# A fused attention and mixture kernel: copies and casts of the first heads on other engines, a new plan, pools in another order

## The chip, the cores and the metric

The kernel runs on one core of one Trainium2 chip. Times are device microseconds of one execution. The kernel before took 740.96 us (median of 3 runs, 740.37 to 741.18). A profile was taken of one more execution; all rows below are from it.

## The reference

Three stages follow each other. The input has 4 batches of 8 heads, 576 tokens, head size 64.

```python
scores = scale * np.matmul(q, k.transpose(0, 1, 3, 2))
bias = -(cum[:, :, :, None] - cum[:, :, None, :])      # cum: running sum of max(s, 0)
scores = np.where(causal, -1e9, scores + np.minimum(bias, 0.0))
attn = np.exp(scores - scores.max(-1)); attn /= attn.sum(-1) + 1e-9
x = (attn @ v), heads side by side                     # 2304 tokens x 512
h = np.maximum(np.maximum(x @ w1, x @ w2), x @ w3)     # 768 columns
x = h @ w_out                                          # 512 columns
e_idx = argmax(x @ w_gate + modality_bias[modality_id])
out[mask] = gate_w[mask] * (np.maximum(x[mask] @ w1[e], 0) @ w2[e])   # 8 experts, 1024 columns
```

All matmuls work with split numbers: a value is a rounded high part (fp32r) and the rest as a low part, and three matmuls (high by high, low by high, high by low) make one product.

## The kernel before, in words

**Attention.** The 32 heads go one after the other, two of them (a pair) sharing one product with v. For each head: k and q come by DMA (L357, L358); their high parts are cast on ScalarE (`k_high` L386, `q_high` L389), k is copied to a second tile on GpSimd (`k_again` L392), the low parts are subtracted (`k_low` L396 on VectorE for head 0 and else on GpSimd, `q_low` L399 on GpSimd, tile q_b). TensorE makes the scores in six blocks (L406, L407), VectorE adds the mask and finds the least (L415), ScalarE takes exp (L422). TensorE then turns the probabilities in four banks of PSUM (L427), and each bank is copied to a tile pt in SBUF (`turned` L432), on VectorE for the (bank, head of the pair) pairs in `PT_V`, on ScalarE for the others: four and four of a pair's eight. The pair's product with v (L462, called pv here) goes to PSUM and is scaled into x (L468, L472).

**Fills.** Between these, TensorE gets pieces of the next stage: for later batches a part of the product of x with w1, w2, w3 is made during attention. A piece is three matmuls (L248, L249, L250; 288 columns); four pieces make one block of PSUM (two banks are there for them), which ScalarE copies (L501) or VectorE takes the maximum of (L503); a transfer h_d<-h (L506) writes the result to DRAM. What isn't made between the heads is made behind the last head.

**The order of the attention stage** is written by a planner, `planned()`: every step is a job with an engine, a guess of its time in ns (`SC_NS`, `PT_NS` and the like), what it waits for and which buffers it takes; among the jobs that could start soon on an engine the one with the lowest key goes first. A key is head x `KEY["T"]` plus a number for the kind of step. The jobs are issued in that order, engine by engine, and each engine works in order.

**Conversion of weights.** The 24 blocks of w1, w2, w3 and w_out come as 64-bit numbers (L212, 512 KB) and are converted: a shift of exponents on ScalarE (L224), three steps on VectorE (L226, L228, L230), a cast to the high part w_h (L235 on ScalarE), the low part w_l by subtraction (L237). Nine are jobs of the planner. The other 15 (`convert_rest`) are written behind the attention; their tiles are in the pools w2p and w1p, their raw data in rawp and raw2. These, and all that follows, are put in order by the framework's own scheduler.

**Behind attention** the first product goes on in six windows of 384 tokens (`stage_a`: L248 to L250 with 384 columns, copies L708, L709, L710, split L714, L715 into tiles fh, fl of the pool hp; x is split at L686, L687 into the pool xsp), then w_out (L724 to L726), routing, and the experts. Their pools are opened after those of attention are closed, on the same memory, one behind the other in the order in which they are written; a tile that lies over a tile of attention waits until that one was last used. The pools of attention lie in the order fxp (12 tiles xh, xl of the fills), fhp (2 tiles h of the fills), qkp (k and q), at1 (mask, q_b, e), vp, ss, tp (pt). The pools behind it are x2p, hmp, jkp, rp, mtp, unp, w2p, xsp, w1p, raw2, hp.

Of the kernel before, what the change touches and what calls it, by code (L numbers as in the profile page):

```python
# [16 lines left out]
T = B * S  # L17
# [64 lines left out]
MIN_NS = {(0, 0): 145, (1, 0): 278, (2, 0): 410, (3, 0): 545, (4, 0): 375, (4, 1): 400}  # L82
SC_NS = {(0, 0): 224, (1, 0): 224, (2, 0): 298, (3, 0): 408, (4, 0): 266, (4, 1): 266}
PT_NS = {"ACT": [420, 420, 275, 485], "DVE": [540, 540, 340, 605]}
CK_POOL = ()
KL_DVE = (0,)
C_ORDER = [(4, 0), (3, 0), (4, 1), (2, 0), (1, 0), (0, 0)]
T_ORDER = [1, 0, 3, 2]
PT_V = [(1, 0), (3, 0), (0, 1), (2, 1)]
CONV = [(0, 3), (1, 3), (2, 5), (3, 7), (4, 7), (5, 9), (6, 13), (7, 15), (8, 17)]  # L90
W_READY, SET_H = 15000, 24
WIRE_FROM, WIRE_TO, WIRE_SLOW = 1300, 900, 1.0
KEY = {"s3": 42741, "T": 27649, "wl": -69055, "wz": -30147, "w1": 173831, "wd": 76793, "ws": 297833, "lx": 64832, "lv": 72681, "ck": -58191, "kb": -116628, "kl": 170828, "ql": -15070, "s": 62000, "mn": 34943, "ex": 51, "ds": 799, "t": 1582, "dt": 3342, "cp": -245871, "r1": -66726, "r2": -76846, "rt": -27814, "rc": -105783, "rw": -81963, "pv": -100422, "x": 41915, "xc": 72719, "xs": 121384, "fe": 59240}
R_MOE1 = (2, 4, 7)
R_MOE2 = (1, 3, 5)

# [84 lines left out]
def fused_kernel(tc, qk, vd, sd, w64, mod, wg, wgt, mb, we, cst, csi, out):  # L181
# [3 lines left out]
    with top:  # L185
# [73 lines left out]
        with ExitStack() as es:  # L259
# [85 lines left out]
            def job(name, run, eng, ns, key, **k):  # L345
                j = Job(run, eng, ns, key, **k)
                jobs.append(j)
                st[name] = j
                return j

            def at(h, what, n=0):
                return h * KEY["T"] + KEY[what] + n

# [47 lines left out]
            def scores(h, c, k):  # L401
                hl, k_b, q_b = tl["hl", h], tl["k_b", h], qbs[h % QB_N]
                q0, w = QC[c][0], QC[c][2]
                k0, n = (k * 288, 288) if c == 4 else (0, w)
                s_ps = tl["s_ps", h, c, k] = ps_s.tile([128, 512], F32, name="s_ps")[:, 0:n]
                P.matmul(s_ps, hl[:, 1, q0:q0 + 128], hl[:, 0, k0:k0 + n], start=True, stop=False)  # L406
                P.matmul(s_ps, q_b[:, q0:q0 + 128], k_b[:, k0:k0 + n], start=False, stop=True)  # L407
# [21 lines left out]
            def turned(h, i):  # L429
                pt = tl["pt", h, i] = tp.tile([128, 512], F32, tag="pt", name="pt", bufs=PT_BUFS)  # L430
                a, z = BANKS[i][1:]
                (V.tensor_copy if (i, h % 2) in PT_V else A.copy)(out=pt[:, a:z], in_=tl["t_ps", h, i][:, a:z])  # L432

            def sums(p):
                r = tl["r", p] = ss.tile([128, 10], F32, name="r")
# [84 lines left out]
            for h in range(2 * NP):  # L520
# [15 lines left out]
                ex = {}  # L536
                for n, (c, k) in enumerate(C_ORDER):
                    bank = Slot("s")
                    a = job(("s", h, c, k), lambda h=h, c=c, k=k: scores(h, c, k), "PE", SC_NS[c, k] + 40, at(h, "s", n * KEY["ds"]), after=[kl, cq, kb, ql, lk], takes=[bank], uses=[s_h, s_q, s_k], tail=210)
                    a = job(("mn", h, c, k), lambda h=h, c=c, k=k: least(h, c, k), "DVE", MIN_NS[c, k], at(h, "mn", n * KEY["ds"]), after=[a] + ([st["mn", h, *C_ORDER[0]]] if n else []), takes=[s_e] if n == 0 else [], uses=[bank, s_e], lag=145 * k)  # L540
                    if k or c < 4:
                        ex[c] = job(("ex", h, c), lambda h=h, c=c: expo(h, c), "ACT", EXP_NS[c], at(h, "ex", n * KEY["ds"]), after=[a], uses=[s_e], tail=0)
                done += ex.values()
                for n, i in enumerate(T_ORDER):
                    bank, s_t = Slot("t"), Slot("pt")
                    turns = job(("t", h, i), lambda h=h, i=i: turn(h, i), "PE", 109 * len(BANKS[i][0]) - 82, at(h, "t", n * KEY["dt"]), after=[ex[c] for c in sorted({c for c, _ in BANKS[i][0]})] + [turns] * (turns is not None), takes=[bank], uses=[s_e], tail=247)
                    eng = "DVE" if (i, j) in PT_V else "ACT"
                    s_p.append((s_t, job(("cp", h, i), lambda h=h, i=i: turned(h, i), eng, PT_NS[eng][i], at(h, "cp", n * KEY["dt"]), after=[turns], takes=[s_t], uses=[bank])))
                if j:
                    bank, s_r, s_0, s_o = Slot("t"), Slot("rb"), Slot("t"), Slot("o")  # L550
# [38 lines left out]
        rp = top.enter_context(tc.tile_pool(name="rp", bufs=2, reuse_waits="tile"))  # L589
        mtp = top.enter_context(tc.tile_pool(name="mtp", bufs=N_EARLY + 2, reuse_waits="tile"))  # L590
        unp = top.enter_context(tc.tile_pool(name="unp", bufs=1, reuse_waits="tile"))
        w2p = top.enter_context(tc.tile_pool(name="w2p", bufs=12, reuse_waits="tile"))
        xsp = top.enter_context(tc.tile_pool(name="xsp", bufs=2, reuse_waits="tile"))
        w1p = top.enter_context(tc.tile_pool(name="w1p", bufs=W1_BUFS, reuse_waits="tile"))
        raw2 = top.enter_context(tc.tile_pool(name="raw2", bufs=R2_BUFS, reuse_waits="tile"))
        hp_ = top.enter_context(tc.tile_pool(name="hp", bufs=1, reuse_waits="tile"))
        ps_a = top.enter_context(tc.tile_pool(name="ps_a", bufs=5, space=PSUM, reuse_waits="tile"))
        ps_b = top.enter_context(tc.tile_pool(name="ps_b", bufs=2, space=PSUM, reuse_waits="tile"))
        ps_r = top.enter_context(tc.tile_pool(name="ps_r", bufs=1, space=PSUM, reuse_waits="tile"))
# [465 lines left out]
```

## Time and profile before

| what | value |
|---|---|
| median of 3 runs | 740.96 us |
| profiled execution, its own time | 743.25 us |
| span in its profile, first to last instruction | 741.5 us |
| mean granted clock of TensorE | 0.990 |
| TensorE matmul rows, share of the span | 97% |
| VectorE, ScalarE, GpSimd, shares of the span | 67%, 55%, 30% |
| attention with its fills ends | some 267 us after the start |

PE is TensorE's matmul row, PEld its weight loads, DVE VectorE, ACT ScalarE, POOL GpSimd, SP the engine that issues most transfers. A q behind a name is the engine's queue of instructions.

### The profile page before, as it was taken

What the parts mean: (1) busy time and instruction counts of PE and PEld (TensorE: products, weight loads), DVE (VectorE), ACT (ScalarE), POOL (GpSimd) and SP (SyncE); (2) the same over time, 40 slices, a digit from 0 to 9 for tenths busy, and PEclk for the clock granted to TensorE, in tenths of its full rate; (3) what the DMA queues carried; (4) which work ended last, traced back from release to release, by engine and by line L of the source; (5) the groups of instructions that cost most, each with busy time, mean ns of one, the idle gap of its engine ahead of it and who ended that gap; (6) DMA issues with size and microseconds to landing.
All of it is one profiled execution on the core that took longest, in us unless ns stands there. A gap on an engine that the chain in (4) does not pass through costs nothing. (4 is left out here: it accounts for less than half of the span.)

```text
span 741.5 us, 13641 instructions
## 1 busy us (share of the span) xinstructions
PE 715.7 (97%) x4602; PEld 639.0 (86%) x4602; DVE 495.2 (67%) x1536; ACT 404.7 (55%) x992; POOL 224.4 (30%) x233
## 2 busy tenths in 40 slices
PE   4999999999999998999999999999999999999996
PEld 4787888778899997999999998999899988999885
DVE  5878988786641158969687796765776566575540
ACT  6999999898721134522222222546555665565531
POOL 7688879766201200000010111032221212222101
PEclk9999999999999999999999999999999999999999
DMA  7576666763131004411101011668478565666610
GB/s 213 152 204 194 205 189 193 198 178 113 64 122 43 31 23 151 146 67 13 53 12 64 23 49 51 202 164 274 123 233 276 203 233 194 233 215 213 226 44 19
DMA packets 43535, 103.83 MB, mean 140 GB/s; under 512 B 9472, under 2 KB 13472, under 8 KB 43456
## 3 DMA queue, kind: packets, MB, share of 16 engines
q1 hardware_dynamic: 35808, 86.04, 37.3%
q0 software_dynamic: 4912, 11.82, 5.0%
q10 hardware_dynamic: 2736, 5.01, 1.8%
q8 instruction: 38, 0.62, 0.4%
q14 instruction: 41, 0.34, 0.2%
HBM read 88.83 MB, written 12.18 MB: 136 GB/s over the span
## 5 line engine op out<-in xcount | busy, mean ns | idle before, releaser
L248 PE MATMUL a_ps<-xh,w_h 128*128 128x384 f32 (+2 forms) x492 | 159.7, 327 | 2.1 <-ACT w_h L235 1.5
L250 PE MATMUL a_ps<-xh,w_l 128*128 128x384 f32 (+2 forms) x492 | 156.9, 320 | 1.6 <-DVE w_l L237 1.4
L249 PE MATMUL a_ps<-xl,w_h 128*128 128x384 f32 (+2 forms) x492 | 156.5, 319 | 0.0
L767 DVE TENSOR_TENSOR e_l<-e_raw,e_h 128x512 fp32r<-128x512 f32 x160 | 104.0, 689 | 11.4 <-ACT e_h L766 10.1
L766 ACT CAST e_h<-e_raw 128x512 fp32r<-128x512 f32 x160 | 93.0, 622 | 14.0 <-DMA e_raw<-in_we 6.0
L248 PEld LDWEIGHTS a_ps<-xh,w_h 128*128 128x128 f32 x492 | 92.8, 189 | 4.4 <-ACT w_h L235 1.9
L250 PEld LDWEIGHTS a_ps<-xh,w_l 128*128 128x128 f32 x492 | 93.0, 189 | 3.3 <-DVE w_l L237 2.8
L249 PEld LDWEIGHTS a_ps<-xl,w_h 128*128 128x128 f32 x492 | 93.2, 189 | 1.0 <-POOL xl L490 0.2
L675 POOL DMA_INDIRECT table<-meta,si x18 | 19.4, 1080 | 244.7 <-DVE nm L663 149.6
L422 ACT ACTIVATE e<-e,mn 128x448 f32<-128x448 f32 (+4 forms) x160 | 88.4, 555 | 4.2 <-DVE mn L415 4.2
L797 PE MATMUL h_ps<-x2t,e_h 128*128 128x256 f32 x288 | 81.1, 282 | 0.0
L798 PE MATMUL h_ps<-x2t,e_l 128*128 128x256 f32 x288 | 81.0, 282 | 0.0
L796 PE MATMUL h_ps<-x2t,e_h 128*128 128x256 f32 x288 | 80.6, 283 | 0.0
L427 PE MATMUL t_ps<-ident,e 128*128 128x128 f32 x480 | 73.5, 288 | 2.8 <-DVE pt L432 2.0
L406 PE MATMUL s_ps<-hl 128*128 128x288 f32 (+1 forms) x192 | 66.7, 357 | 7.8 <-DVE hl L396 7.1
L650 DVE CUSTOM_DVE_ANT_0 junk<-x,wg 128x512 bf16<-128x512 f32 x96 | 66.0, 687 | 11.8 <-ACT x L728 11.0
L415 DVE CUSTOM_DVE_ANT_0 e<-s_ps,mask 128x288 f32<-128x288 f32 (+4 forms) x160 | 63.2, 423 | 14.2 <-PE s_ps L407 13.1
L427 PEld LDWEIGHTS t_ps<-ident,e 128*128 128x128 f32 x480 | 58.8, 148 | 7.7 <-DVE pt L432 2.7
L407 PE MATMUL s_ps<-k_b,q_b 66*128 66x288 f32 (+1 forms) x192 | 59.6, 323 | 4.6 <-DMA k_b<-augk 3.3
L826 PE MATMUL y_ps<-e_h,gh 128*128 128x512 f32 x152 | 61.5, 405 | 0.4 <-ACT gh L818 0.4
L828 PE MATMUL y_ps<-e_h,gl 128*128 128x512 f32 x152 | 60.8, 400 | 0.0
L827 PE MATMUL y_ps<-e_l,gh 128*128 128x512 f32 x152 | 60.1, 395 | 0.0
(178 smaller groups left out, 1488.8 us busy)
## 6 DMA issues: line engine op xcount, KB each, us to landing
e_raw<-in_we SPq DMA_DIRECT2D x80, 512.0 KB
w_raw<-in_w SPq DMA_DIRECT2D x24, 512.0 KB
qk_r<-in_qk SPq DMA_DIRECT2D x31, 288.0 KB
v_r<-in_vd SPq DMA_DIRECT2D x16, 320.0 KB
rb<-r_d SPq DMA_DIRECT2D x32, 160.0 KB
qk_r<-in_qk SPq DMA_DIRECT2D x32, 144.0 KB
x2d<-x ACTq DMA_DIRECT2D x18, 256.0 KB
w_h<-w_z POOLq DMA_DIRECT2D x9, 256.0 KB, 3.8
```

The costliest lines, as they stand in the source:

```text
L248: P.matmul(a_ps, wh[:, c], xh, start=c == 0, stop=False)
L249: P.matmul(a_ps, wh[:, c], xl, start=False, stop=False)
L250: P.matmul(a_ps, wl[:, c], xh, start=False, stop=c == 3)
L406: P.matmul(s_ps, hl[:, 1, q0:q0 + 128], hl[:, 0, k0:k0 + n], start=True, stop=False)
L422: A.activation(out=ec, in_=ec, func=ACTF.Exp, bias=tl["mn", h][:, c:c + 1], scale=-1.0, accum_out=tl["l", p][:, j, c:c + 1])
L427: P.transpose(out=t_ps[:, n * 128:(n + 1) * 128], in_=e_bufs[h % E_N][:, EOFF[c] + kb * 128:EOFF[c] + (kb + 1) * 128], identity=ident)
L650: V.tensor_tensor_reduce(out=junk, in0=x2, in1=wg_sb[ei // 2][:, ei % 2, :], scale=1.0, scalar=0.0, op0=ALU.mult, op1=ALU.add, accum_out=l ...
L766: A.copy(out=h, in_=raw[:, a])
L767: V.tensor_tensor(out=lo, in0=raw[:, a], in1=h.bitcast(F32), op=ALU.subtract)
L796: P.matmul(h_ps, w(hs, f, c), xt[:, 0, c], start=c == 0, stop=False)
L797: P.matmul(h_ps, w(hs, f, c), xt[:, 1, c], start=False, stop=False)
L798: P.matmul(h_ps, w(ls, f, c), xt[:, 0, c], start=False, stop=c == 3)
```

## The change

Three things change. For the first six heads two more banks of each pair, (0, 0) and (1, 1), are copied by VectorE, so six of eight. The cast of k for heads 3 and 5 goes from ScalarE to GpSimd. The planner's table of keys is another one, and its guess for the scores is 30 ns longer; so all steps of attention are ordered anew. The pools behind attention lie in another order: hp and xsp come before w2p, and hp no longer last.

```diff
-CK_POOL = ()
+CK_POOL = (3, 5)
...
+PT_EARLY, PT_W = 6, [(0, 0), (1, 1)]
...
-KEY = {"s3": 42741, "T": 27649, "wl": -69055, "wz": -30147, "w1": 173831, "wd": 76793, "ws": 297833, "lx": 64832, "lv": 72681, "ck": -58191, "kb": -116628, "kl": 170828, "ql": -15070, "s": 62000, "mn": 34943, "ex": 51, "ds": 799, "t": 1582, "dt": 3342, "cp": -245871, "r1": -66726, "r2": -76846, "rt": -27814, "rc": -105783, "rw": -81963, "pv": -100422, "x": 41915, "xc": 72719, "xs": 121384, "fe": 59240}
+KEY = {"s3": 262888, "T": 15750, "wl": 29386, "wz": 48740, "w1": 225687, "wd": 68498, "ws": 411529, "lx": 95995, "lv": 209700, "ck": 138477, "kb": -116340, "kl": -53033, "ql": -58361, "s": 115494, "mn": -5610, "ex": 153024, "ds": 361, "t": 18694, "dt": 19213, "cp": -53151, "r1": -208485, "r2": -212716, "rt": 15596, "rc": -242689, "rw": 44183, "pv": -165391, "x": -56845, "xc": 100720, "xs": -74110, "fe": -88191}
...
-                (V.tensor_copy if (i, h % 2) in PT_V else A.copy)(out=pt[:, a:z], in_=tl["t_ps", h, i][:, a:z])
+                (V.tensor_copy if (i, h % 2) in PT_V or h < PT_EARLY and (i, h % 2) in PT_W else A.copy)(out=pt[:, a:z], in_=tl["t_ps", h, i][:, a:z])
...
-                    a = job(("s", h, c, k), lambda h=h, c=c, k=k: scores(h, c, k), "PE", SC_NS[c, k] + 40, at(h, "s", n * KEY["ds"]), after=[kl, cq, kb, ql, lk], takes=[bank], uses=[s_h, s_q, s_k], tail=210)
+                    a = job(("s", h, c, k), lambda h=h, c=c, k=k: scores(h, c, k), "PE", SC_NS[c, k] + 70, at(h, "s", n * KEY["ds"]), after=[kl, cq, kb, ql, lk], takes=[bank], uses=[s_h, s_q, s_k], tail=210)
...
-                    eng = "DVE" if (i, j) in PT_V else "ACT"
+                    eng = "DVE" if (i, j) in PT_V or h < PT_EARLY and (i, j) in PT_W else "ACT"
...
         unp = top.enter_context(tc.tile_pool(name="unp", bufs=1, reuse_waits="tile"))
+        hp_ = top.enter_context(tc.tile_pool(name="hp", bufs=1, reuse_waits="tile"))
+        xsp = top.enter_context(tc.tile_pool(name="xsp", bufs=2, reuse_waits="tile"))
         w2p = top.enter_context(tc.tile_pool(name="w2p", bufs=12, reuse_waits="tile"))
-        xsp = top.enter_context(tc.tile_pool(name="xsp", bufs=2, reuse_waits="tile"))
         w1p = top.enter_context(tc.tile_pool(name="w1p", bufs=W1_BUFS, reuse_waits="tile"))
         raw2 = top.enter_context(tc.tile_pool(name="raw2", bufs=R2_BUFS, reuse_waits="tile"))
-        hp_ = top.enter_context(tc.tile_pool(name="hp", bufs=1, reuse_waits="tile"))
```

One line comes in near the top, so a step at line n of before is at n + 1 in the changed kernel.

On ScalarE, behind the last copy of probabilities (pt): before, the copies of the fills (L501) and of the first projected block (L708) come first, and then the first cast of the 15 conversions (w_h).

```order
L432 COPY pt<-t_ps 128x512
L686 CAST xh<-x_2825 128x384 x4
L501 COPY h<-a_ps 128x288
L486 CAST xh<-x_1270 128x288 x2
L486 CAST xh<-x_2066 128x288 x2
L501 COPY h<-a_ps 128x288 x3
L486 CAST xh<-x_2066 128x288 x4
L501 COPY h<-a_ps 128x288 x2
L486 CAST xh<-x_2066 128x288 x2
L501 COPY h<-a_ps 128x288 x2
L708 COPY h<-a_ps 128x384 x2
L235 CAST w_h<-w_z 128x512
```

The same place in the changed kernel:

```order
L433 COPY pt<-t_ps 128x512
L236 CAST w_h<-w_z 128x512 x2
L225 ACTIVATE w_z<-w_raw 128x512 x2
L236 CAST w_h<-w_z 128x512
L502 COPY h<-a_ps 128x288
L687 CAST xh<-x_2875 128x384
L236 CAST w_h<-w_z 128x512
L487 CAST xh<-x_1269 128x288 x2
L225 ACTIVATE w_z<-w_raw 128x512
L487 CAST xh<-x_2055 128x288 x2
L236 CAST w_h<-w_z 128x512
```

The conversions moved in among the fills' copies; all 15 casts w_h stand ahead of the copy of the first projected block.

On VectorE, from the last pair's x to the first maximum of a projected block (L709), before:

```order
L468 TENSOR_TENSOR x_2825<-o_ps,rb 128x512
L503 TENSOR_TENSOR h<-a_ps,h 128x288
L472 TENSOR_TENSOR x_2825<-t_ps,rb 128x64
L687 TENSOR_TENSOR xl<-x_2825,xh 128x384
L503 TENSOR_TENSOR h<-a_ps,h 128x288 x17
L709 TENSOR_TENSOR h<-a_ps,h 128x384 x2
```

The end of the same stretch in the changed kernel:

```order
L231 SCALAR_TENSOR_TENSOR w_z<-w_raw,w_z 128x512
L504 TENSOR_TENSOR h<-a_ps,h 128x288
L227 TENSOR_SCALAR w_z<-w_z 128x512
L238 TENSOR_TENSOR w_l<-w_z,w_h 128x512
L229 SCALAR_TENSOR_TENSOR w_z<-w_raw,w_z 128x512
L231 SCALAR_TENSOR_TENSOR w_z<-w_raw,w_z 128x512
L504 TENSOR_TENSOR h<-a_ps,h 128x288 x2
L238 TENSOR_TENSOR w_l<-w_z,w_h 128x512
L504 TENSOR_TENSOR h<-a_ps,h 128x288 x4
L710 TENSOR_TENSOR h<-a_ps,h 128x384 x2
```

Seventeen evictions of fills stood by themselves; now the steps of the conversions stand between them, and four evictions follow the last w_l.

On GpSimd, at the start of attention, with buffer numbers (q_b0 to q_b2 are of heads 0 to 2, hl_194 is head 1's, hl_204 head 2's), before:

```order
L399 TENSOR_TENSOR q_b0_124<-qk_r_169,hl_182 64x576
L399 TENSOR_TENSOR q_b1_125<-qk_r_174,hl_194 64x576
L399 TENSOR_TENSOR q_b2_126<-qk_r_177,hl_204 64x576
L396 TENSOR_TENSOR hl_194<-qk_r_174,hl_194 64x576
L396 TENSOR_TENSOR hl_204<-qk_r_177,hl_204 64x576
L392 CAST k_b_228<-qk_r_177 64x576
L396 TENSOR_TENSOR hl_276<-qk_r_213,hl_276 64x576
```

and now (hl_274 is head 3's):

```order
L400 TENSOR_TENSOR q_b0_124<-qk_r_169,hl_182 64x576
L400 TENSOR_TENSOR q_b1_125<-qk_r_174,hl_194 64x576
L397 TENSOR_TENSOR hl_194<-qk_r_174,hl_194 64x576
L400 TENSOR_TENSOR q_b2_126<-qk_r_177,hl_204 64x576
L397 TENSOR_TENSOR hl_204<-qk_r_177,hl_204 64x576
L387 CAST hl_274<-qk_r_213 64x576
L393 CAST k_b_228<-qk_r_177 64x576
L397 TENSOR_TENSOR hl_274<-qk_r_213,hl_274 64x576
```

Head 1's low half of k moved ahead of head 2's q_b, and the cast of k for head 3 has come in. On TensorE, counted in the order: ahead of the sixteenth pv stand 67 pieces of fills before and 71 now.

## Rows read from the trace of the kernel before

**Rows 1.** The page, part 1: busy us, share of span, instructions of each engine.
```profile
PE 715.7 (97%) x4602; PEld 639.0 (86%) x4602; DVE 495.2 (67%) x1536; ACT 404.7 (55%) x992; POOL 224.4 (30%) x233
```

**Rows 2.** Windows: length, busy us (instructions) of PE, PEld, DVE, ACT, POOL; clock, DMA.
```profile
20.00:60.00 40.00, 38.43 (x256) 30.16 (x254) 33.40 (x115) 37.32 (x107) 30.50 (x29) 0.91 0.62 170
60.00:213.00 153.00, 149.17 (x1150) 124.72 (x1149) 120.71 (x405) 132.04 (x386) 102.71 (x91) 0.99 0.55 161
213.00:268.00 55.00, 54.41 (x389) 52.31 (x388) 11.12 (x25) 8.84 (x24) 7.78 (x10) 1.00 0.18 61
```

**Rows 3.** Windows of 10 us behind the fills, the same columns.
```profile
280.00:290.00 10.00, 7.98 (x43) 7.02 (x41) 8.09 (x15) 4.70 (x9) 0.00 (x0) 0.98 0.48 158
290.00:300.00 10.00, 8.92 (x40) 8.13 (x41) 9.00 (x18) 5.44 (x9) 0.00 (x0) 0.84 0.51 156
```

**Rows 4.** Groups by line of PE, 268 to 301: busy, mean ns, idle before.
```profile
L248 PE MATMUL a_ps<-xh,w_h 128*128 128x384 f32 x52 | 18.4, 353 | 2.0 <-ACT w_h L235 1.5 <-ACT h L708 0.5
L250 PE MATMUL a_ps<-xh,w_l 128*128 128x384 f32 x51 | 18.2, 357 | 1.6 <-DVE w_l L237 1.4
L249 PE MATMUL a_ps<-xl,w_h 128*128 128x384 f32 x52 | 18.0, 346 | 0.0
```

**Rows 5.** Timeline of PE: start us, length, instruction; two of 45 close starts.
```profile
268.19 0.34 PE L249 MATMUL a_ps<-xl,w_h 128*128 128x384 f32 x1
...
275.96 0.34 PE L248 MATMUL a_ps<-xh,w_h 128*128 128x384 f32 x1
```

**Rows 6.** Timeline of ACT: first copy of a projected block, first cast w_h, fh0.
```profile
267.37 0.86 ACT L708 COPY h<-a_ps 128x384 f32<-128x384 f32 x2 [2.71 <-PE a_ps L249]
271.60 0.62 ACT L235 CAST w_h<-w_z 128x512 fp32r<-128x512 f32 x1 [3.36 <-DMA h_d<-h]
272.12 0.51 ACT L714 CAST fh<-h 128x384 fp32r<-128x384 f32 x1
```

**Rows 7.** Groups of DVE by shape, 280 to 300: the conversion's steps.
```profile
L228 DVE SCALAR_TENSOR_TENSOR w_z<-w_raw,w_z 128x512 int32<-128x512 int32 x6 | 4.1, 689 | 0.1
L237 DVE TENSOR_TENSOR w_l<-w_z,w_h 128x512 fp32r<-128x512 f32 x6 | 4.1, 688 | 0.3 <-ACT w_h L235 0.2
...
L226 DVE TENSOR_SCALAR w_z<-w_z 128x512 int32<-128x512 int32 x6 | 2.6, 425 | 1.9 <-ACT w_z L224 1.8
```

**Rows 8.** Groups by shape, 213 to 268: VectorE's evictions of fills.
```profile
L503 DVE TENSOR_TENSOR h<-a_ps,h 128x288 f32<-128x288 f32 x18 | 8.2, 458 | 41.9 <-PE a_ps L250 33.7 <-issue 5.2 <-ACT h L501 3.0
```

**Rows 9.** Timeline of DVE: the last pair's x, and the xl behind it.
```profile
216.99 0.21 DVE L472 TENSOR_TENSOR x<-t_ps,rb 128x64 f32<-128x64 f32 x1
217.78 0.56 DVE L687 TENSOR_TENSOR xl<-x,xh 128x384 fp32r<-128x384 f32 x1 [0.58 <-ACT xh L686]
```

**Rows 10.** Groups of ACT, 264 to 302: the conversion's steps.
```profile
L235 ACT CAST w_h<-w_z 128x512 fp32r<-128x512 f32 x10 | 6.2, 618 | 7.2 <-DVE w_z L230 3.7 <-DMA h_d<-h 3.4
L224 ACT ACTIVATE w_z<-w_raw 128x512 f32<-128x512 f32 x9 | 6.1, 677 | 6.6 <-DVE w_l L237 3.6 <-DMA w_raw<-in_w 3.0
```

**Rows 11.** Groups of DVE by shape, 20 to 200: a conversion step during attention.
```profile
L228 DVE SCALAR_TENSOR_TENSOR w_z<-w_raw,w_z 128x512 int32<-128x512 int32 x11 | 14.7, 1344 | 0.1
```

**Rows 12.** Groups by shape, 20 to 60: the copies and casts that change engine.
```profile
L392 POOL CAST k_b<-qk_r 64x576 fp32r<-64x576 f32 x8 | 6.3, 797 | 0.2
L386 ACT CAST hl<-qk_r 64x576 fp32r<-64x576 f32 x7 | 4.7, 669 | 0.2
...
L432 DVE COPY pt<-t_ps 128x448 f32<-128x448 f32 x6 | 3.7, 623 | 1.7 <-PE t_ps L427 1.2 <-ACT e L422 0.5
L432 ACT COPY pt<-t_ps 128x448 f32<-128x448 f32 x5 | 2.6, 523 | 0.8 <-PE t_ps L427 0.8
```

**Rows 13.** Waits, 20 to 60: who, for whom, us in total, times, longest.
```profile
POOL hl L396 <- ACT hl L386: 6.9, 3, 4.7
```

**Rows 14.** Timeline of POOL: low halves of k, heads 1 and 2.
```profile
12.20 2.79 POOL L396 TENSOR_TENSOR hl<-qk_r,hl 64x576 fp32r<-64x576 f32 x2
```

**Rows 15.** Timeline of PE: head 1's first block of scores.
```profile
14.00 0.58 PE L406 MATMUL s_ps<-hl 128*128 128x288 f32 x1
```

## The prediction

> **What bounds the kernel now.** I read the page first, then the stretches in windows, then who waited for whom in the two places where the windows show a loss. By the page TensorE's matmul row is busy 97% of the span [rows 1], so a first guess is that nothing on the other engines matters. The windows correct that. From 213 to 268 us the matmuls stand close while VectorE works 11.1 us of 55 and ScalarE 8.8 [rows 2]; this is the stretch in which the fills that are left run by themselves. Straight behind it, in 280 to 300, the number of matmuls falls to 43 and 40 in 10 us while VectorE works 8.1 and 9.0 us [rows 3]. So the kernel has 55 us with two nearly empty engines, and then a place where TensorE waits for just these two.
>
> How much is lost there? Between 268 and 301 us the three lines of the projection ran 52 + 51 + 52 = 155 matmuls of 384 columns [rows 4]. Close together they start 0.177 us apart: two starts 44 matmuls apart are 275.96 - 268.19 = 7.77 us [rows 5]. 155 x 0.177 = 27.4 us of 33, so 5.6 us are lost. The releasers named are the weights' conversion, w_h on ScalarE and w_l on VectorE [rows 4]; at the same place the granted clock is 0.84 in one window [rows 3], a part of it at the lower level, 1.2 GHz in place of 2.4.
>
> Here the measure decides the size. The busy shares of the matmul row in 280 to 300 leave 20 - 7.98 - 8.92 = 3.1 us [rows 3]; counted, it is 5.6. The Trainium skill (Perfetto Trace Analysis, "Identifying the Most-Contended Engine") says that matmul busy time is no good measure and points to the LDWEIGHTS busy share instead. By that share (7.02 + 8.13 in the two windows [rows 3], against 52.3 of 55 in the fills [rows 2], 9.5 in each) the loss would be 3.9 us, and my sum would end 1.7 us higher. The trace agrees on the first half of the rule; on the second the count of matmuls says more, because a load at the lower clock is itself longer.
>
> Why were the conversions late? ScalarE's first w_h stands at 271.60 and had waited 3.36 us for the landing of a fill's transfer h_d<-h [rows 6], issued at the end of the last fill. The first tile of the pool w2p lies over memory of the fills' last tiles. Since ScalarE works in order, all 15 conversions that the planner doesn't hold stand behind it.
>
> **The change part by part.** *Pools in another order.* hp and xsp now lie where w2p began, and w2p over tiles that the last heads free. The order shows what this lets loose: in ScalarE's row all 15 casts w_h now stand ahead of the copy of the first projected block, where before all stood behind it. The 5.6 us go; ends 3.1 (busy shares) and 5.6. What is late next is the fills' own end: fh0 now lies where that last fill tile was, and needs the landing that released the cast at 271.60; its cast stood at 272.12 anyway, behind that one [rows 6], so this costs nothing.
>
> The conversions now share VectorE's row with the evictions of the fills. From the last pair's x to the last w_l the new row has 13 w_l, 12 + 11 of the two three-operand steps, 11 shifts and 12 fill evictions: 13 x 0.688 + 23 x 0.688 + 11 x 0.425 [rows 7] + 12 x 0.458 [rows 8] + one xl 0.56 [rows 9] = 35.5 us. Behind it stand four evictions of VectorE, so six of fills, each 12 matmuls, 1.7 us at the 389 in 55 us of [rows 2]: 10.2 us. Together 45.7 us, against the 50 us that TensorE's own work took there before, from x at 217.2 [rows 9] to the first projected copy at 267.4 [rows 6]. ScalarE adds 15 x 0.618 + 13 x 0.677 = 18.1 us [rows 10] to 8.8 of 55 and isn't near. If VectorE runs without a gap, TensorE waits for nothing; if it is kept at 85%, as in 280 to 300 (17.1 of 20 [rows 3]), 35.5 / 0.855 + 10.2 = 51.7, 1.7 us too many. Ends 0 and 10 (the step that takes 689 ns there took 1344 on average in the attention stage [rows 11]; 11 x 0.655 = 7.2 more, also at 85%). I take +1.0: GpSimd's work beside it is 7.8 us of 55 [rows 2].
>
> That 1344 has a rule beside it that speaks against the change. The Trainium skill (SBUF — State Buffer, "Who interferes with whom") says that a VectorE instruction with two inputs in SBUF contends with GpSimd instructions that read SBUF. By it each of the fills' ten xl on GpSimd would meet a conversion; the doubled step in attention agrees. If all ten cost the 0.65 us, the 45.7 us would be 52.2, and the sum would end 2.2 us higher than at no gap.
>
> *Copies and casts of the first six heads.* Six copies of 448 columns leave ScalarE, 6 x 0.523 = 3.1 us, and cost VectorE 6 x 0.623 = 3.7; two casts of k leave ScalarE, 2 x 0.669 = 1.3, and cost GpSimd 2 x 0.797 = 1.6 [rows 12]. In 20 to 60 us ScalarE was the fullest, 37.3 of 40, VectorE 33.4, GpSimd 30.5 [rows 2]. Now ScalarE has 32.9, VectorE 37.1, GpSimd 32.1: the place of the fullest engine changes hands and its load falls 0.2 us. What falls more is a wait: GpSimd stood 6.9 us for ScalarE's cast of k [rows 13], and it now makes two of these casts itself; TensorE in turn waits there for q_b. At best the 40 us shrink to 37.1 (a gain of 2.9), by loads at equal filling 0.2, and at worst the copies all stand in VectorE's chain, 3.7 lost. I take a gain of 1.0, nearer to the loads.
>
> *The start.* Head 1's low half of k now stands ahead of the third q_b on GpSimd. Before, it was the first of two from 12.20 to 14.99, so done at 13.6 [rows 14]; TensorE took up head 1 at 14.00 [rows 15], 0.4 behind it, so this was hardly what it waited for. One step less in front of it is 1.4 us, the upper end; the lower is nothing. I take 0.2, next to the lower.
>
> *The rest of the new plan.* From 60 to 213 us 149.2 of 153 us are busy and the clock is 0.99 [rows 2]; little is left to take. By the new order the sixteenth pv has 71 pieces of fills in front of it (67 before), each three matmuls or 0.4 us at that rate: 1.6 us of holes filled, if the heads keep their pace. I take half, 0.8. Ends: 5 either way, the clock's 1.5 us (1% of 153) and the 3.8 us not busy.
>
> *The sum:* -5.6 + 1.0 - 1.0 - 0.2 - 0.8 = -6.6 us. The profiled execution took 743.25, so 736.6 for one like it; the median of the runs is 2.3 lower, 740.96, which gives **734.4 us**.
>
> **The rivals.** *The gain is taken back in the fills.* A fill's eviction behind a conversion that waits for its load holds TensorE, which has two banks for fills. For: VectorE's row has up to six conversion steps between two evictions, some 3.7 us, while a bank is wanted every 1.7. Against: 4 us of spare by the sum. Price 4 to 9 us: at 6.5 net of 1.0 the time is 739.9.
>
> *The plan gives more than I grant.* The clock in 20 to 60 was 0.91 [rows 2], so 3.6 us at full speed were not granted; if the waits for q_b go and the lower level with them, 3.6 in place of 1.0, and the filled holes give 1.6: 734.4 - 3.4 = 731.0. Against: VectorE at 37.1 is as full as ScalarE was.
>
> *Slower: VectorE paces the first heads.* It keeps its 6.6 us of waiting in those 40 [rows 2], and the 3.7 us of copies come on top; each late copy holds a bank that TensorE's next turn wants, and a second stretch at the lower clock like the present one costs another 3.6. 7.3 us lost in place of 1.0 gained: 734.4 + 8.3 = 742.7. It decides from the point where VectorE's idle time in that window stays over 3 us.
>
> *The pools don't do what they say.* If another late tile (the last pair's pt, freed at 217) lies under the weights, the conversions start some us later but still inside the stretch; only if the chain stays whole are the 5.6 back: 740.96 - 2.0 = 739.0.
>
> **How the numbers follow.** 0.2% of 741 is 1.5 us, about what a measurement can tell from no change: faster is below 739.5, slower above 742.4. My forecast, 732 to 738, has 0.54; the plan giving more 0.20; fills taking it back 0.12, half of it below 739.5; pools without effect 0.05, mostly below; slower by VectorE 0.09, most of it above 742.4. So faster 0.54 + 0.20 + 0.06 + 0.03 = 0.83, the same 0.09, slower 0.08. The range leaves out the upper part of the last two and the far end of the second: 729.5 to 740.3; the forecast's own is 732 to 738.
>
> **What would show it.** Right: ScalarE's casts w_h between about 213 and 258 us, none behind 268; 57 or so matmuls of 384 columns in every 10 us behind the fills, at clock 1.00; VectorE 40 to 47 us busy in the fills' stretch; GpSimd's wait for ScalarE's cast down from 6.9 us. Wrong: waits of TensorE for a_ps evictions of a us and more between 213 and 265, new windows with a clock under 0.9 before 213, or an x of the last pair later than 217 by more than 2 us.

## The result, and the profile after

The changed kernel took 734.3 us (median of 4 runs, 733.24 to 734.66) against 740.82 of the kernel before beside it: ratio 0.9912, 95% interval 0.9892 to 0.9932. Once more beside the experiments it took 735.0 us against 741.88, ratio 0.9925 (0.9898 to 0.9953). The forecast of 734.4 was met. The experiments below show that its parts were not: the pools gave less than their term and the plan more, so the sum was met in part by luck.

The profiled execution has a span of 732.2 us. In windows (span, then busy time and instructions of PE, PEld, DVE, ACT, POOL, then the granted clock, the DMA share and GB/s), the changed kernel reads, against [rows 2, 3]:

```profile
20.00:60.00 40.00, 36.82 (x264) 28.48 (x262) 37.22 (x126) 36.10 (x107) 33.92 (x31) 1.00 0.65 185
60.00:213.00 153.00, 151.25 (x1183) 125.95 (x1183) 120.12 (x412) 132.03 (x383) 98.61 (x90) 1.00 0.54 157
213.00:268.00 55.00, 53.10 (x369) 51.92 (x368) 40.41 (x77) 22.53 (x45) 9.37 (x10) 1.00 0.51 169
240.00:250.00 10.00, 8.20 (x57) 7.37 (x56) 9.90 (x17) 5.79 (x12) 4.18 (x4) 1.00 0.55 188
268.00:301.00 33.00, 33.00 (x182) 31.55 (x182) 10.43 (x24) 7.72 (x20) 0.00 (x0) 1.00 0.03 7
280.00:290.00 10.00, 10.00 (x60) 10.00 (x59) 2.55 (x5) 1.99 (x4) 0.00 (x0) 1.00 0.04 11
```

Behind the fills TensorE is now full at clock 1.00: 60 matmuls in 280 to 290, where it was 43. In exchange VectorE's work between 213 and 268 went from 11.1 to 40.4 us, and there is a new loss in 240 to 250: VectorE works 9.90 of 10 us and TensorE 8.20.

ScalarE's timeline (start, duration, instruction, in brackets the wait ahead of it and what ended it): the last cast w_h, the first projected copy, and the cast of fh0, to be laid beside [rows 6]:

```profile
254.57 0.62 ACT L236 CAST w_h<-w_z 128x512 fp32r<-128x512 f32 x1
264.18 0.88 ACT L709 COPY h<-a_ps 128x384 f32<-128x384 f32 x2 [2.28 <-PE a_ps L250]
268.83 0.51 ACT L715 CAST fh<-h 128x384 fp32r<-128x384 f32 x1 [3.77 <-DMA h_d<-h]
```

The wait for the landing of h_d<-h is still there, but it has moved from the first weight cast to fh0. No weights stand behind it any more, and it costs TensorE nothing: its row is busy 33.00 of 33 us from 268 on.

In the new hole TensorE's waits of 0.1 us and more are these:

```profile
241.36 0.40 PE L249 MATMUL a_ps<-xh,w_h 128*128 128x288 f32 x1 [0.16 <-ACT h L502]
245.70 0.40 PE L249 MATMUL a_ps<-xh,w_h 128*128 128x288 f32 x1 [1.12 <-DVE h L504]
248.48 0.40 PE L249 MATMUL a_ps<-xh,w_h 128*128 128x288 f32 x1 [0.52 <-ACT h L502]
```

VectorE's timeline in front of the longest of them shows why the eviction (L504) was late:

```profile
242.62 0.45 DVE L504 TENSOR_TENSOR h<-a_ps,h 128x288 f32<-128x288 f32 x1
242.98 1.07 DVE L238 TENSOR_TENSOR w_l<-w_z,w_h 128x512 fp32r<-128x512 f32 x1
243.98 1.29 DVE L231 SCALAR_TENSOR_TENSOR w_z<-w_raw,w_z 128x512 int32<-128x512 int32 x1
245.20 0.44 DVE L504 TENSOR_TENSOR h<-a_ps,h 128x288 f32<-128x288 f32 x1
245.57 0.65 DVE L227 TENSOR_SCALAR w_z<-w_z 128x512 int32<-128x512 int32 x1
246.14 1.29 DVE L238 TENSOR_TENSOR w_l<-w_z,w_h 128x512 fp32r<-128x512 f32 x1
247.35 0.68 DVE L229 SCALAR_TENSOR_TENSOR w_z<-w_raw,w_z 128x512 int32<-128x512 int32 x1
```

And this is GpSimd in the same time (one group of four):

```profile
242.70 4.18 POOL L491 TENSOR_TENSOR xl<-x,xh 128x288 fp32r<-128x288 f32 x4 [20.35 <-ACT xh L487]
```

From 242.70 to 246.88 GpSimd subtracts xl, and in just this time VectorE's w_l and three-operand steps (L238, L229, L231), 0.68 to 0.69 us each before and after it, take 1.07 to 1.29.

In 20 to 60 us the waits (engine, line, what it waited for: sum, times, longest) answer to [rows 13]; two more of before, and then three of now:

```profile
POOL q_b L399 <- ACT hl L389: 1.1, 1, 1.1
PE s_ps L407 <- POOL q_b L399: 1.0, 1, 1.0
```

```profile
POOL q_b L400 <- ACT hl L390: 4.7, 1, 4.7
PEld s_ps L407 <- DVE mn L416: 2.0, 2, 1.6
PE s_ps L407 <- DVE mn L416: 1.6, 2, 1.4
```

GpSimd's wait of 6.9 us for ScalarE's cast of k is gone, but its wait for ScalarE's cast of q has grown from 1.1 to 4.7 us. TensorE, which waited 1.0 us for q_b, now waits 1.6 us for VectorE's least values; VectorE is the fullest engine there, 37.2 of 40.

### The profile page after: what moved, and what is told of

The parts are those of the page before. It is cut to its first block, busy times and chain, and to the rows that moved or that the text cites. A ratio compares the mean times of both kernels' runs of the same rounds, so it can differ in the third digit from the quotient of the medians.

```text
span 732.2 us, 13634 instructions
## 1 busy us (share of the span) xinstructions
PE 708.2 (97%) x4602; PEld 633.5 (87%) x4602; DVE 497.4 (68%) x1542; ACT 399.9 (55%) x984; POOL 225.3 (31%) x235
## 5 line engine op out<-in xcount | busy, mean ns | idle before, releaser
L428 PE MATMUL t_ps<-ident,e 128*128 128x128 f32 x480 | 70.1, 280 | 1.4 <-DVE pt L433 0.6
L408 PE MATMUL s_ps<-k_b,q_b 66*128 66x288 f32 (+1 forms) x192 | 57.9, 317 | 4.1 <-DMA k_b<-augk 3.9
L428 PEld LDWEIGHTS t_ps<-ident,e 128*128 128x128 f32 x480 | 56.0, 143 | 5.7 <-DVE pt L433 2.0
```

The costliest lines, as they stand in the source:

```text
L428: P.transpose(out=t_ps[:, n * 128:(n + 1) * 128], in_=e_bufs[h % E_N][:, EOFF[c] + kb * 128:EOFF[c] + (kb + 1) * 128], identity=ident)
```

## The experiments

Twelve runs followed (ten other kernels, one of them twice, and the changed kernel again), each beside the kernel before, whose medians in the three sets were 740.95, 741.88 and 741.27 us; so across sets ratios are compared.

| kernel | median, us | ratio (95%) | x of last pair | to first projected copy | from there to the end |
|---|---|---|---|---|---|
| before (profile of the first part) | 740.96 | | 215.9 | 51.5 | 474.1 |
| changed, first time | 734.3 | 0.9912 (0.9892 to 0.9932) | 212.8 | 51.4 | 468.0 |
| changed, again | 735.0 | 0.9925 (0.9898 to 0.9953) | 213.8 | 51.4 | 468.1 |
| pools only | 740.19 | 0.9995 (0.9981 to 1.0009) | 213.5 | 54.6 | 468.0 |
| plan only | 736.88 | 0.9939 (0.9914 to 0.9963) | 214.4 | 49.5 | 471.7 |
| hp first | 738.76 | 0.9976 (0.9961 to 0.9990) | 212.7 | 55.6 | 468.0 |
| xsp first | 744.94 | 1.0052 (1.0026 to 1.0077) | 215.7 | 56.9 | 472.1 |
| last six held back | 733.03 | 0.9903 (0.9875 to 0.9931) | 211.7 | 49.0 | 467.9 |
| the same again | 733.11 | 0.9885 (0.9867 to 0.9903) | 214.9 | 49.0 | 468.1 |
| all 15 spread | 735.03 | 0.9925 (0.9899 to 0.9951) | 210.0 | 53.1 | 467.8 |
| w_l on GpSimd | 742.65 | 1.0018 (1.0000 to 1.0036) | 215.8 | 57.9 | 468.6 |
| copies, old keys | 751.63 | 1.0140 (1.0121 to 1.0160) | 224.4 | 57.6 | 468.3 |
| new keys, copies of two heads | 742.13 | 1.0014 (1.0001 to 1.0028) | 219.7 | 51.9 | 467.9 |
| old plan, last six held back | 736.52 | 0.9943 (0.9923 to 0.9963) | 215.7 | 51.2 | 468.1 |

The last three columns are of one profiled execution each: the start of the last pair's x (L468 or L469) on VectorE, the time from it to ScalarE's first copy of a projected block, and from that to the span's end. One execution can lie well off its kernel's median (below), so small differences in these columns count only where several kernels agree.

**Pools only.** The four pool lines of the change in the kernel before, nothing else:

```diff
+        hp_ = top.enter_context(tc.tile_pool(name="hp", bufs=1, reuse_waits="tile"))
+        xsp = top.enter_context(tc.tile_pool(name="xsp", bufs=2, reuse_waits="tile"))
         w2p = top.enter_context(tc.tile_pool(name="w2p", bufs=12, reuse_waits="tile"))
-        xsp = top.enter_context(tc.tile_pool(name="xsp", bufs=2, reuse_waits="tile"))
...
-        hp_ = top.enter_context(tc.tile_pool(name="hp", bufs=1, reuse_waits="tile"))
```

> The kernel before with the new order of the pools alone; keys, copies and casts as before. Theory (the first weight tile lay over the fills' last tile, so the pools alone set the conversions free): all casts w_h before 268 us; the stretch from the first projected copy to the end, 474.1 us before and 468.0 after, comes to 468 here too, and the conversions cost 0 to 3 us among the fills: 735 to 738. Rival 1 (the gain behind the fills needs the new plan's timing): 739.5 or more, stretch above 472. Rival 2 (the pools did nothing, the keys everything): 741.

A miss in the time: 740.19, no difference that can be measured. The mechanism is there, 468.0 us from the first projected copy to the end as foreseen. But the stretch in front of it is 3.1 us longer than before:

```profile
213.00:268.00 55.00, 51.81 (x363) 50.60 (x362) 38.19 (x70) 21.85 (x43) 9.07 (x10) 1.00 0.50 166
240.00:250.00 10.00, 8.22 (x59) 7.54 (x58) 9.93 (x17) 5.52 (x11) 4.21 (x4) 1.00 0.57 187
```

The gain is made behind the fills and given back among them, where VectorE is full (9.93 of 10) and TensorE waits. This is the rival "the gain is taken back in the fills", which had 739.9; with the old plan it is what happens. The columns alone don't make up the median, though: 6.1 us won and 3.1 lost leave 3.0, and the medians differ by 0.8. The profile here is of the fastest of the twelve executions (737.90 us), and that of before is of one 2.3 us above its median (743.25 against 740.96).

**Plan only.** The changed kernel with the old order of the pools (the same lines the other way).

> The changed kernel with the pools in the old order: new keys, copies and casts alone. Theory: the casts w_h stand behind the last fill's landing again, the stretch from the first projected copy to the end is 473 to 475 us as before, and attention is 1 to 3.2 us shorter: 737.5 to 740. Rival 2 (the keys did it all): 734 to 736. Rival 3 (the plan is worth nothing alone, or a loss; the clock spells of the profiled kernel before were chance): 740.5 to 742.

736.88, a little better than the theory's best. The conversions are late again; ScalarE's and TensorE's timelines (one fence each) show it:

```profile
263.91 0.86 ACT L709 COPY h<-a_ps 128x384 f32<-128x384 f32 x2 [2.56 <-PE a_ps L250]
266.39 0.62 ACT L236 CAST w_h<-w_z 128x512 fp32r<-128x512 f32 x1 [1.62 <-DMA h_d<-h]
```

```profile
284.84 0.44 PE L251 MATMUL a_ps<-xh,w_l 128*128 128x384 f32 x1 [0.66 <-DVE w_l L238]
290.52 0.44 PE L251 MATMUL a_ps<-xh,w_l 128*128 128x384 f32 x1 [0.74 <-DVE w_l L238]
```

From the copy to the end it takes 471.7 us, 3.7 more than with the new pools, where before it was 474.1: the same late conversions cost less here.

**hp first, xsp first.** In the kernel before, one pool alone is moved ahead of w2p.

```diff
+        hp_ = top.enter_context(tc.tile_pool(name="hp", bufs=1, reuse_waits="tile"))
         w2p = top.enter_context(tc.tile_pool(name="w2p", bufs=12, reuse_waits="tile"))
...
-        hp_ = top.enter_context(tc.tile_pool(name="hp", bufs=1, reuse_waits="tile"))
```

> The kernel before with hp alone put ahead of w2p (xsp stays behind w2p). Theory: only what lies over the fills' last tile counts. Now that is fh0, whose cast needs that landing anyway, so this is as good as the whole new order: within 1 us of the run with pools only, 735 to 738, fh0's cast still waiting some 3 to 4 us for the transfer. Rival (the place of xsp, w1p and raw2 matters too): 739 or more.

738.76, 0.8 above what the theory gave, but that range was too low already for the pools-only run. hp alone is 1.4 us below the whole new order, but the two intervals overlap (0.9961 to 0.9990 and 0.9981 to 1.0009), so it isn't shown to be better. fh0 waits for the landing as foreseen, and it is 468.0 us from the first copy to the end: the place over the fills' last tile is all that counts there.

```profile
272.32 0.51 ACT L714 CAST fh<-h 128x384 fp32r<-128x384 f32 x1 [3.09 <-DMA h_d<-h]
```

In the other kernel xsp takes that place:

```diff
+        xsp = top.enter_context(tc.tile_pool(name="xsp", bufs=2, reuse_waits="tile"))
         w2p = top.enter_context(tc.tile_pool(name="w2p", bufs=12, reuse_waits="tile"))
-        xsp = top.enter_context(tc.tile_pool(name="xsp", bufs=2, reuse_waits="tile"))
```

> The kernel before with xsp alone put ahead of w2p (hp stays last). Theory: the first split of x now lies over the fills' last tile and has to wait for its landing near 271 us; the weights are converted early, but no projection can be made before the split, so TensorE stands 4 to 6 us with nothing to do behind the last fill: 739.5 to 743, that is 4 to 6 us slower than with hp in that place. Rival (it is enough that w2p leaves the place): 735 to 738, no such wait.

744.94, 2 us past the theory's upper end: the wait was there, shorter for TensorE than the 4 to 6 us foreseen, and on top the fills lost time as in the other kernels with new pools. ScalarE's row shows the same landing now holding the split of x, and TensorE's row the wait that follows from it:

```profile
266.28 1.75 ACT L686 CAST xh<-x 128x384 fp32r<-128x384 f32 x4 [4.56 <-DMA h_d<-h]
```

```profile
266.85 1.13 PE L248 MATMUL a_ps<-xh,w_h 128*128 128x384 f32 x5 [2.90 <-ACT xh L686]
```

So the wait belongs to the place in memory, and it goes to whichever tile lies there; the kernels differ in what has to wait with it. The 2.90 us are not the whole loss of this kernel: in its profile TensorE also waited among the fills, 1.61 us for a copy on ScalarE and 1.45 for GpSimd's xl, and had the lower clock for a while:

```profile
240.00:250.00 10.00, 7.97 (x47) 7.50 (x46) 8.61 (x14) 3.96 (x8) 3.35 (x3) 0.83 0.52 173
```

**The changed kernel again, and its conversions paced.** Four kernels in one set.

> The changed kernel once more, beside the runs that follow, since the runs of the two halves came to -0.8 us (pools alone) and -4.1 us (plan alone) and not to the -4.6 and -2.0 of the prediction. If the halves add up, 740.9 - 4.9 = 736.0; if they help each other, 734.3 as the first time, and the span has no more than one spell at the lower clock before 268 us.

735.0. By the ratios the halves add up to 4.9 us (0.05% and 0.61% of 741); the whole is worth 5.6 by this ratio (0.75%) and 6.5 by the first (0.88%). The intervals are 1 to 2 us wide on each side, so whether the halves help each other stays open. This execution had the lower clock in 32 to 39 us, which the first did not have (below).

The pacing holds the first shift of a late conversion behind a chosen eviction of the fills, by an edge that orders the two on VectorE (`evs` lists the evictions):

```diff
+        evs = []
...
-                    V.tensor_tensor(out=tl["h", i, f], in0=a_ps, in1=tl["h", i, f], op=ALU.max)
+                    evs.append(V.tensor_tensor(out=tl["h", i, f], in0=a_ps, in1=tl["h", i, f], op=ALU.max).ins)
...
-            V.tensor_scalar(out=zi, in0=zi, scalar1=3, scalar2=None, op0=ALU.logical_shift_left)
+            if early or ({0: -4, 1: -2}.get(f, -1) if k == 3 else None) is None:
+                V.tensor_scalar(out=zi, in0=zi, scalar1=3, scalar2=None, op0=ALU.logical_shift_left)
+            else:
+                with tc.issue_after(evs[({0: -4, 1: -2}.get(f, -1) if k == 3 else None)]):
+                    V.tensor_scalar(out=zi, in0=zi, scalar1=3, scalar2=None, op0=ALU.logical_shift_left)
```

> The changed kernel with the last six conversions (w_out, wanted only from some 300 us on) held back on VectorE by edges of order: their first shift stands behind the 4th, 2nd and last of the fills' last evictions. Theory (VectorE is too dense in 230 to 250, so evictions come late and TensorE stands 2.9 us): TensorE's idle time in 240 to 250 falls from 2.9 to 1.5 or less, nothing is lost behind 268, 732 to 733.5. Rival (the time is lost to GpSimd's xl or to ScalarE's copies, not to the density of VectorE): no change, 734.3. Rival (what is held back is late again behind the fills): 735 to 737, with waits on w_l L238 in 280 to 300.

733.03, as the theory had it. In windows:

```profile
240.00:250.00 10.00, 9.91 (x74) 9.56 (x74) 1.83 (x4) 2.23 (x6) 3.11 (x4) 1.00 0.09 31
268.00:301.00 33.00, 33.00 (x187) 31.28 (x186) 18.57 (x43) 9.84 (x23) 0.00 (x0) 1.00 0.13 47
```

The hole in 240 to 250 is closed (74 matmuls in place of 57; 0.09 us of the matmul row idle in place of 1.80, where the expectation had 2.9). VectorE's steps of the six conversions now run from 255 to 277 us, three of their w_l behind 268, and cost TensorE nothing there. The stretch from x to the copy falls from 51.4 to 49.0 us.

> The changed kernel with the last six conversions held back, once more, to settle by how much it beats the changed kernel: 733.0 the first time against 735.0. Theory: 732.5 to 733.5, idle time of TensorE in 240 to 250 at 0.5 us again. Rival (a matter of the spells at the lower clock in few runs): 734 to 735.

733.11, and again 49.0 and 468.1 us. This version beats the kernel before clearly. Against the changed kernel the intervals of single sets overlap (0.9867 to 0.9903 here, 0.9892 to 0.9932 and 0.9898 to 0.9953 there); all runs of both together, ten with a median of 733.0 against eleven with 734.6, put it some 2 us ahead, and both pairs of profiles have the 2.4 us from x to the copy.

The next one spreads all 15, with the index -17 + 1.4 x the conversion's number, rounded down, for the nine of w1, w2 and w3, and min(-1, -4 + f) for those of w_out.

> The changed kernel with all 15 conversions spread evenly over the fills' evictions, one conversion to one or two evictions of VectorE. Theory: TensorE's idle time between 213 and 268 falls from 3.4 to 1 us or less, nothing is lost behind: 731.5 to 732.5, the best of these. Rivals as for the spread of the last six: 734.3, or 735 to 737 with waits on w_l behind 268.

A miss: 735.03, no better than the changed kernel. The releaser is GpSimd now; first TensorE's timeline, then GpSimd's:

```profile
244.29 0.40 PE L256 MATMUL a_ps<-xl,w_h 128*128 128x288 f32 x1 [1.51 <-POOL xl L497]
```

```profile
240.05 4.19 POOL L497 TENSOR_TENSOR xl<-x,xh 128x288 fp32r<-128x288 f32 x4 [19.84 <-PE a_ps L256]
```

VectorE has conversion steps in just that time, and they take nearly twice their 0.68 to 0.69 us:

```profile
241.08 1.30 DVE L237 SCALAR_TENSOR_TENSOR w_z<-w_raw,w_z 128x512 int32<-128x512 int32 x1
242.30 1.29 DVE L235 SCALAR_TENSOR_TENSOR w_z<-w_raw,w_z 128x512 int32<-128x512 int32 x1
```

With the last six held back the same four xl took 3.11 us, here 4.19 beside conversions. So a smaller number of conversion steps between evictions is not enough. In the better kernel no conversion step stands on VectorE between 237 and 255, and so none beside these xl (240.79 to 243.90); that this is what helps is read from the two traces and not tested by itself.

The low parts on GpSimd:

```diff
-            (G if early else V).tensor_tensor(out=lo, in0=z, in1=h.bitcast(F32), op=ALU.subtract)
+            G.tensor_tensor(out=lo, in0=z, in1=h.bitcast(F32), op=ALU.subtract)
```

> The changed kernel with the low parts w_l of the 15 late conversions on GpSimd instead of VectorE: 15 x 0.69 = 10 us leave VectorE, and GpSimd gets 15 x 1.4 = 20 us of two-input work on SBUF beside it. Theory (the contention rule: VectorE's steps with two SBUF inputs grow while GpSimd reads): the steps L229 and L231, 0.73 to 0.78 us now, come to 0.95 or more, and most of the 10 us are eaten again; idle time of TensorE in 230 to 250 stays at 1 to 4 us, 733 to 736. Rival (no contention worth the name): steps at 0.69 to 0.75, the idle time gone, 731.5 to 732.5.

742.65, slower than theory and rival. The groups of VectorE between 205 and 268 us (busy, mean ns):

```profile
L231 DVE SCALAR_TENSOR_TENSOR w_z<-w_raw,w_z 128x512 int32<-128x512 int32 x13 | 15.5, 1192 | 0.3
L229 DVE SCALAR_TENSOR_TENSOR w_z<-w_raw,w_z 128x512 int32<-128x512 int32 x13 | 10.4, 804 | 0.3
```

One of the two steps grew as the theory said (1.19 us; 0.77 in the changed kernel), the other hardly (0.80 from 0.73). The part that I had not foreseen: the fills' xl queue behind the w_l on GpSimd, and TensorE waits for them three times (1.05, 0.86 and 0.69 us, ending at 251.7, 255.1 and 264.8), besides two waits of 1.2 us for evictions on VectorE; x to copy is 57.9 us. VectorE's share of this isn't parted from GpSimd's.

**The old plan with the last six held back.** The pools-only kernel with the same edges of order.

> The kernel before with the new pools and the last six conversions held back as in the run that spread them; keys, copies and casts as before. Theory (with pools alone the 6 us won behind the fills are lost again among them, 6.1 us of idle time in 210 to 270 against 1.9, because VectorE and GpSimd are crowded there): idle time falls to 2 to 3.5 us, 736.5 to 738 against 740.2. Rival (the loss there is the old plan's own and not that of crowding): 739.5 to 741.

736.52 and 51.2 us from x to copy, where pools only had 54.6:

```profile
240.00:250.00 10.00, 10.00 (x76) 9.81 (x75) 1.96 (x5) 2.50 (x6) 3.09 (x4) 1.00 0.24 81
```

The idle time of the matmul row in 213 to 268 falls from 3.19 us (51.81 of 55 above) to 0.79. So it was the crowding that ate the pools' gain: on the old plan they are worth nothing that can be measured with it, and 0.57% (0.9943), 4.2 us, without it.

**Copies and casts without the keys, keys without the copies.** The first has the new pools, the copies and the casts, but the old `KEY` and `SC_NS + 40`; the second is the changed kernel with

```diff
-CK_POOL = (3, 5)
+CK_POOL = ()
-PT_EARLY, PT_W = 6, [(0, 0), (1, 1)]
+PT_EARLY, PT_W = 2, [(0, 0), (1, 1)]
```

> The pools in the new order and the six of eight copies on VectorE and the two casts on GpSimd, with the old keys and the old guess for the scores: against the run with pools only (740.2) this shows the copies and casts alone. Theory of the prediction (loads of ScalarE and VectorE change places): 1 us gained, 739.2. Rival 1 (copies and casts carry all of the plan's 4.1 us): 736. Rival 2 (VectorE paces the first heads and the old keys are not made for it): 742 or more.

751.63: the second rival's "742 or more", and far beyond it. The window of 20 to 60 us, and TensorE's longest wait from there to the last pair's x:

```profile
20.00:60.00 40.00, 35.28 (x218) 27.75 (x218) 33.65 (x114) 33.44 (x100) 31.76 (x28) 0.87 0.60 175
```

```profile
179.09 0.40 PE L249 MATMUL a_ps<-xh,w_h 128*128 128x288 f32 x1 [4.08 <-DVE h L504]
```

None of the engines is full in that window, and VectorE with 33.65 of 40 doesn't pace it, yet TensorE makes 38 matmuls fewer than before [rows 2]: this points to the order, which was made for other loads, though no run here changes the old order by itself. From 172.3 to 178.6 VectorE fills tables that the planner had put there, ahead of an eviction. The four runs also have the lowest clocks of all, 0.982 to 0.988. These are some places out of several; the whole of the 11 us is not taken apart.

> The changed kernel with the additional copies on VectorE for the first two heads only instead of six, and all casts of k on ScalarE; new keys and pools (with no such copies at all the planner finds no order). Theory (the copies and casts relieve ScalarE in heads 2 to 5): against 735.0 of the changed kernel 1 to 3 us slower, 736 to 738, with GpSimd waiting for ScalarE's cast of k again. Rival (the keys carry the plan's gain by themselves): 734.5 to 735.5.

742.13, 4 us beyond the theory and far from the rival. GpSimd's wait for ScalarE's cast of k is back, in 20 to 60 us:

```profile
POOL hl L397 <- ACT hl L387: 8.1, 2, 6.5
```

Whether the four heads' copies or the two casts are what is missed, this kernel doesn't part, and its profile also has the lower clock at 140 to 160 us (0.74 and 0.92). Neither half of the plan is a gain by itself here: copies without keys cost some 11 us against pools only, keys with few of the copies and without the casts 7 us against the changed kernel.

## Why the prediction was right in its sum and wrong in its parts

*The pools, -5.6.* Right in mechanism; the size holds for the profiled execution and was too large for the runs. From the first projected copy to the end 474.1 became 468.0, 6.1 us, and every kernel with early conversions has 467.8 to 468.6, save the one whose split waits. By the count of matmuls the loss was 5.6, by the LDWEIGHTS share (the Trainium skill, Perfetto Trace Analysis, "Identifying the Most-Contended Engine") 3.9; for this execution the count was nearer. But some of the 6.1 came with the lower clock at 289 us [rows 3]: 0.98 and 0.84 over 20 us are 1.8 us not granted. The plan-only kernel, with late conversions and clock 1.00 in 280 to 300, loses 3.7, and the pools on the old plan, with the crowding gone, gave 4.2 us in the runs (2.7 to 5.7 by the interval).

*The fills, +1.0.* Mis-sized. The step was "45.7 us against the 50 us", so four to spare. Measured from x to copy: +3.1 us for the pools in the old plan, +1.9 in the new one (51.4 against 49.5). A sign of being wrong that the prediction had named, a wait of a us and more for an eviction, did come (1.12 us at 245.70). The sum over 50 us hid that the conversions don't spread over it: all casts stand between 208 and 255, VectorE is at 9.9 of 10 in 240 to 250 and mostly idle from 257 on. The contention that the prediction set beside the sum (the Trainium skill, SBUF — State Buffer, "Who interferes with whom": two SBUF inputs on VectorE against GpSimd's reads) is in the rows: 0.69 to 1.07 and 1.29 us, and GpSimd's four xl 4.18 in place of 3.11. By it the sum stood 2.2 us above one without a gap, nearer to what was measured than the +1.0 that I took. Holding back the last six conversions takes the loss away, which shows that crowding is its cause; how much is contention and how much plain density the runs don't part.

*Copies and casts -1.0, start -0.2, the rest of the plan -0.8.* Too small, and wrong in kind. The plan alone gave 0.61%, 4.5 us, not 2.0. What the three terms are worth singly the runs don't show, but one part is firm: from x to the copy the new plan needs some 2 us less, 49.5 against 51.5 with the old pools and 49.0 against 51.2 with the last six held back. These are the four pieces, 12 matmuls, that stand ahead of x: 1.6 by the prediction, of which it took half. Behind the copy plan only loses 2.4 us less than the profile of before, which was in no term; up to 1.8 of it is the lower clock at 289 us. That its last x comes 1.5 us earlier than before proves little: one and the same old plan put the last x anywhere from 212.7 to 215.9 us in five profiles, and the new one from 211.7 to 215.8 in six (the run with all 15 spread aside). And the terms do not exist singly: the copies were priced by the loads of the engines, at an order of steps that no longer held. VectorE's load in 20 to 60 came out as worked out (37.2, forecast 37.1), but by the two kernels that part copies from keys, what the loads are worth the order decides.

*The sum.* The pools net were forecast at -4.6 and gave -1 to -2 on the new plan (ratios 0.9939 against 0.9925 and 0.9912, with intervals that overlap) and next to nothing on the old one; the plan was forecast at -2.0 and gave -4.5. The two errors have opposite signs, and so 734.4 was met: the sum is partly luck. "VectorE paces the first heads" did come true in the row of waits, without its price. What the new wait costs against the one it replaced isn't shown: in 20 to 60 us TensorE made 264 matmuls at clock 1.00, but in the second profile, at 0.91 as before, 255 where before had 256.

## What to carry to other kernels

A tile that lies over a late buffer stalls its whole in-order queue; put there a tile behind which nothing urgent stands in that queue. When work is freed to run early, ask where it will crowd: a stretch that has room over 50 us can still be full for 10, and work that isn't wanted yet is better held back. Don't add up terms for an assignment of work and for the order that was made for it; try each alone before either is credited.

## What the runs showed of the hardware that was not expected

The lower clock comes and goes between executions of the same code. In 30 to 40 us the windows of the changed kernel's first profile and of its second read (columns as above):

```profile
30.00:40.00 10.00, 7.82 (x52) 6.36 (x52) 9.54 (x37) 8.19 (x27) 9.57 (x9) 1.00 0.51 148
```

```profile
30.00:40.00 10.00, 8.45 (x42) 7.73 (x43) 8.85 (x33) 7.98 (x26) 8.70 (x9) 0.66 0.53 143
```

Ahead of it TensorE had waited for VectorE's least values 1.44 us in the first and 2.26 us in the second:

```profile
31.26 0.30 PE L407 MATMUL s_ps<-hl 128*128 128x64 f32 x1 [1.44 <-DVE mn L416]
```

```profile
30.59 0.30 PE L407 MATMUL s_ps<-hl 128*128 128x64 f32 x1 [2.26 <-DVE mn L416]
```

The same split runs through all seven profiles that have the changed kernel's keys, copies and casts: the three with a wait of 1.42 to 1.44 us there had clock 1.00 in 30 to 40, the four with 2.25 or 2.26 had 0.66. Why the wait is longer in some executions stays open. Two profiles of one kernel, the last six held back, show it too:

```profile
30.21 0.30 PE L413 MATMUL s_ps<-hl 128*128 128x64 f32 x1 [1.44 <-DVE mn L422]
```

```profile
30.11 0.30 PE L413 MATMUL s_ps<-hl 128*128 128x64 f32 x1 [2.26 <-DVE mn L422]
```

A clock of 0.66 over 10 us is 3.4 us of full speed not granted, yet the last pair's x came only 1.0 us later (213.8 against 212.8). Counted from the matmul behind the wait, it is 1.6 us (183.2 in place of 181.6 us to x), since the slower execution had been ahead; so about half of the lower level was hidden. In the other pair, where a second spell (0.91 over 160 to 180) came on top, the same stretch took 184.8 in place of 181.5 us. So of the wait and the clock behind it only a part is ever to be won, and one profile of a kernel isn't its time: the version with the last six held back has spans of 728.6 and 732.0 us, at clocks of 0.998 and 0.992.
